# Part B of a gated two-branch kernel: projections over dense features, with copies between SBUF tiles for the heads

## The chip, the cores and the metric

The kernel runs on one core of one Trainium2 chip. The metric is the device time of one execution in microseconds. The engines are PE (TensorE, with its weight loads shown as PEld), DVE (VectorE), ACT (ScalarE), POOL (GpSimd) and SP (SyncE, which only issues DMAs and waits); ACT issues DMAs too. An engine runs its instructions in order, and so does the queue on which it issues DMAs: a command that waits holds everything behind it on that engine.

## The reference

Two branches over the same `x` (2048 tokens, 640 features) are mixed by a gate.

```python
g = sigmoid((x * gate_w).sum(-1, keepdims=True))
a = A_ref(x, mem0, Wq, Wk, Wv, Wo, seg_len)   # recurrent: 64 segments of 32 tokens, one after the other
b = B_ref(x, wqkv, wo)                        # local attention, dilated
return g * a + (1 - g) * b
```

Only B matters for the change. It has 32 heads of 20 features; each token attends to 8 tokens: itself and every second one before it.

```python
def B_ref(x, wqkv, wo):
    H, Dh, W, dil = 32, 20, 8, 2
    q, k, v = (x @ wqkv) split in three, then in H heads of Dh
    idx = pos[:, None] - (arange(W) * dil)[None, :]       # masked where negative
    logits = einsum('bhsd,bhswd->bhsw', q, k[idx]) * Dh ** -0.5
    attn = softmax(logits)
    o = einsum('bhsw,bhswd->bhsd', attn, v[idx])
    return o.reshape(B, S, 640) @ wo
```

## The kernel before

The program has three stages in this order: part B (`part_b`), a pre-pass for A (`prepass`), and the recurrent part A (`part_a`). Part B writes its result, already multiplied by `1 - g`, to DRAM; part A adds its own and stores the output.

**Part B.** The 2048 tokens are cut into five blocks `b`: four of 484 tokens (four chains `u` of 121 tokens of one parity, so that a dilated window is a band) and a last one of 112. Within a block the 32 heads are taken in eight groups `g` of four. Every array that a group needs has one head per 32 partitions, because PE addresses its tiles at multiples of 32: head `h` of a group lies in partitions 32h to 32h+19, and the other 12 are padding. To get there, the weights are padded: `wqk` holds each head's 20 columns in a slot of 32 (zeros behind them, built by POOL and DVE casts from a raw load), and `wop`, the output weight, has four heads' rows per slot (a POOL memset of the whole tile, then four DMAs of 20 rows).

One step of the loop at the end of `part_b` is one `(b, g)`:

- `proj` of the next group: five matmuls (the five chunks of 128 input features) give q of four padded heads, five more give k; DVE evicts q, ACT k, into `bqT` and `bkT` of three buffers each;
- `scores`: 16 small matmuls, an exp on ACT and a multiply by the band on DVE, in two halves;
- `values` of the group before: 16 matmuls for the sums and 16 for the weighted values; then Ln and Exp on ACT for the reciprocal, and a multiply on DVE that writes `OT`, the transposed output, in which each group again has its slot of 128 rows;
- from time to time `make_xT` (transposes x for the next 512 tokens, computes the gate, lets POOL copy two rearrangements `xh` and `zx` that SP stores to DRAM), `make_v` (v of the next block), and `out_tile`, the output projection of 128 tokens: eight matmuls, one per group, for each half of the columns, evicted by ACT and DVE and stored from ACT's queue.

**What sets the order.** Part B is ordered by a scheduler that places the program's instructions on each engine's list; within an engine and within a DMA queue that order is fixed. DMAs on SP and ACT share eight completion semaphores, taken in turn: a DMA waits until the one that last used its semaphore has landed. `load_early` puts eleven resident weights (`wres_q`, 384 KB each) and three DRAM-to-DRAM copies (`wscr`) on SP's queue after the first store of `xh`. Five streamed weights (`wst`) for the pre-pass follow at 58 us; once part B's buffers come free, `load_late` brings the rest (`wlate_*`). The pre-pass starts with `wres_q` and `wst` (L424).

The change touches L127 to L136 (weight loads and padding), `proj` (L213 to L224), one slice in `scores`, the end of `values` (L267 to L269), `out_tile` (L271 to L283) and the loop's order.

Of the kernel before, what the change touches and what calls it, by code (L numbers as in the profile page):

```python
# [10 lines left out]
BF = mybir.dt.bfloat16  # L11
# [4 lines left out]
N_LATE = 55  # L16
N_LATE2 = 22
WBUFS = 5

_DEV = {"mode": "full"}  # L20

# [3 lines left out]
class _K:  # L25
# [58 lines left out]
    def part_b(self):  # L84

        nc, tc, KC, S = self.nc, self.tc, self.KC, self.S
        NQ, HALO = 121, 14
        BQ = 4 * NQ
# [8 lines left out]
        with ExitStack() as ctx:  # L97
            wp = ctx.enter_context(tc.tile_pool(name="b_w", bufs=1))
            io = ctx.enter_context(tc.tile_pool(name="b_io", bufs=4))
            blkp = ctx.enter_context(tc.tile_pool(name="b_blk", bufs=1))  # L100
            wk = ctx.enter_context(tc.tile_pool(name="b_wk", bufs=2))
# [14 lines left out]
                load_x(i)  # L116
            wv = wp.tile([128, KC, 640], BF, name="wv_sb")
            gw = wp.tile([128, KC, 1], BF, name="gw_sb")
            wop = wp.tile([128, 8, 640], BF, name="wo_pad")
            wqk = [wp.tile([128, KC, 32, 32], BF, name=f"w{n}_pad") for n in "qk"]  # L120
            xT = wp.tile([128, KC, HALO + S], BF, name="xT")
            OT = wp.tile([128, 8, S], BF, name="OT")
            wsrc = self.wqkv.rearrange("(c p) f -> p c f", p=128)
            for n, w in enumerate(wqk):
                nc.gpsimd.memset(w[:, :, :, 20:32], 0.0)
                raw = OT[:].rearrange("p g t -> p (g t)")[:, 3200 * n:3200 * n + 3200]
                (nc.scalar, nc.sync)[n].dma_start(raw.rearrange("p (c f) -> p c f", c=KC), wsrc[:, :, 640 * n:640 * n + 640])  # L127
                for kc in range(KC):
                    eng = (nc.vector, nc.gpsimd)[(KC * n + kc) % 2]
                    eng.tensor_copy(w[:, kc, :, 0:20], raw[:, 640 * kc:640 * kc + 640].rearrange("p (h d) -> p h d", d=20))  # L130
            nc.sync.dma_start(gw[:], self.gate_w.rearrange("(c p o) -> p c o", p=128, o=1))
            nc.scalar.dma_start(wv[:], wsrc[:, :, 1280:1920])
            nc.gpsimd.memset(wop[:], 0.0)
            wosrc = self.wo.rearrange("(g h d) f -> h d g f", h=4, d=20)
            for hh in range(4):
                nc.sync.dma_start(wop[32 * hh:32 * hh + 20, :, :], wosrc[hh])  # L136
            ones = wp.tile([128, 32], BF, name="b_ones")
            nc.vector.memset(ones[:], 1.0)
            band = wp.tile([128, NQ], BF, name="band")
# [57 lines left out]
            def make_v(b):  # L197
                nq, nu, c0 = shape_of(b)
                nk = nq + 7
                for u in range(nu):  # L200
# [8 lines left out]
                        self.evac(V[0:nk, 320 * f:320 * f + 320], ps[0:nk, 0:320])  # L209
                    Vs[b, u] = V  # L210

            qk = {}

            def proj(b, g):
                nq, nu, c0 = shape_of(b)
                nt = nq * nu
                for n, (o0, nn) in enumerate(((c0 + HALO, nt), (c0, nt + HALO))):
                    ps = bank(F32, "ps_bqk")
                    for kc in range(KC):
                        nc.tensor.matmul(ps[:, 0:nn], lhsT=wqk[n][:, kc, 4 * g:4 * g + 4, :].rearrange("p h d -> p (h d)"),  # L220
                                         rhs=xT[:, kc, o0:o0 + nn], start=(kc == 0), stop=(kc == KC - 1))
                    t = wk.tile([128, BQ + HALO], BF, name="b" + "qk"[n] + "T", bufs=3)
                    self.evac(t[:, 0:nn], ps[:, 0:nn], "dve" if n == 0 else "act")
                    qk[b, g, n] = t  # L224

            Ps = {}

            def scores(b, g):
                nq, nu, c0 = shape_of(b)
                nk = nq + 7  # L230
                qT, kT = qk.pop((b, g, 0)), qk.pop((b, g, 1))
                for hp in range(2):
                    ps = psS.tile([128, 2, 512], F32, tag="S", name="ps_bS")
                    for u in range(nu):
                        a = 242 * (u // 2) + u % 2
                        for r in range(2):
                            rs = slice(64 * hp + 32 * r, 64 * hp + 32 * r + 32)
                            nc.tensor.matmul(ps[0:nk, r, nq * u:nq * u + nq], lhsT=kT[rs, a:a + 2 * nk - 1:2],
                                             rhs=qT[rs, a:a + 2 * nq - 1:2], start=(u == 0), stop=(u == nu - 1),
                                             tile_position=(64 * hp + 32 * r, 0), skip_group_check=True)  # L240
                    P = wk.tile([128, 2, BQ], BF, name="bP", bufs=4)
                    Pv = P[0:nk, :, 0:nq * nu]
                    nc.scalar.activation(Pv, ps[0:nk, :, 0:nq * nu], ACT.Exp, scale=scale_b)  # L243
                    P4 = Pv.rearrange("p r (u n) -> p r u n", n=nq)
                    m = band0[0:nk, 0:nu, 0:nq].unsqueeze(1) if b == 0 else \
                        band[0:nk, 0:nq].unsqueeze(1).unsqueeze(1)
                    nc.vector.tensor_tensor(out=P4, in0=P4, in1=m.to_broadcast([nk, 2, nu, nq]), op=ALU.mult)
                    Ps[b, g, hp] = P

            def values(b, g):  # L250
                nq, nu, c0 = shape_of(b)
                nk, nt = nq + 7, nq * nu
                po = psO.tile([128, 512], F32, tag="O", name="ps_bO")
                pz = psO.tile([128, 512], F32, tag="Z", name="ps_bZ")
                P = [Ps.pop((b, g, hp)) for hp in range(2)]
                for u in range(nu):
                    for out, z in ((pz, True), (po, False)):
                        for hh in range(4):
                            h = 4 * g + hh
                            nc.tensor.matmul(out[32 * hh:32 * hh + 32, nq * u:nq * u + nq],  # L260
                                             lhsT=ones[0:nk, :] if z else Vs[b, u][0:nk, 20 * h:20 * h + 32],
                                             rhs=P[hh // 2][0:nk, hh % 2, nq * u:nq * u + nq], start=(u == 0),
                                             stop=(u == nu - 1), tile_position=(0, 32 * hh), skip_group_check=True)
                rz = wk.tile([128, BQ], F32, name="b_rz")
                nc.scalar.activation(rz[:, 0:nt], pz[:, 0:nt], ACT.Ln)
                nc.scalar.activation(rz[:, 0:nt], rz[:, 0:nt], ACT.Exp, scale=-1.0)
                dst = OT[:, g, BQ * b:BQ * b + nt].rearrange("p (l n q) -> p l q n", l=nu // 2, q=2)  # L267
                nc.vector.tensor_tensor(out=dst, in0=po[:, 0:nt].rearrange("p (l q n) -> p l q n", q=2, n=nq),
                                        in1=rz[:, 0:nt].rearrange("p (l q n) -> p l q n", q=2, n=nq), op=ALU.mult)  # L269

            def out_tile(ti):  # L271
                bo = io.tile([128, 640], BF, name="bo", bufs=2)
                for f in range(2):
                    ps = bank(F32, "ps_bo")
                    for g in range(8):
                        nc.tensor.matmul(ps[:, 0:320], lhsT=OT[:, g, 128 * ti:128 * ti + 128],
                                         rhs=wop[:, g, 320 * f:320 * f + 320], start=(g == 0), stop=(g == 7))
                    if f == 0:
                        nc.scalar.activation(bo[:, 0:320], ps[:, 0:320], ACT.Copy, scale=self.omg_sb[:, ti:ti + 1])
                    else:  # L280
                        nc.vector.tensor_scalar(out=bo[:, 320:640], in0=ps[:, 0:320], scalar1=self.omg_sb[:, ti:ti + 1],
                                                scalar2=None, op0=ALU.mult)
                nc.scalar.dma_start(self.bsc_dram[ti * 128:(ti + 1) * 128, :], bo[:])  # L283

            nc.scalar.preload_act_table_set("natural_log_exp_and_others")
            steps = [(b, g) for b in range((S + BQ - 1) // BQ) for g in range(8)]
            self.first_store = None
            make_xT(0)
            with tc.issue_after(self.first_store):
                self.load_early()  # L290
            make_v(0)
            proj(*steps[0])
            ti = 0
            for i, (b, g) in enumerate(steps):
                if g == 2 and b + 1 < S // 512:
                    make_xT(b + 1)
                if (b, g) == (S // 512 - 1, 0):
# [4 lines left out]
                    for n in range(4):  # L302
                        for q in range(4):
                            nc.sync.dma_start(self.gZ[32 * q:32 * q + 32, n:n + 1],
                                                g_dram[:, 24:32, 4 * n + q:4 * n + q + 1])
                if g == 6 and i + 8 < len(steps):
                    make_v(b + 1)
                if i + 1 < len(steps):
                    proj(*steps[i + 1])
                scores(b, g)  # L310
                if i > 0:
                    values(*steps[i - 1])
                if g >= 1 and b > 0 and 128 * (ti + 1) <= BQ * b:
                    out_tile(ti)
                    ti += 1
            values(*steps[-1])
# [602 lines left out]
```

## Time and profile before

| | |
|---|---|
| median of 3 runs | 1776.31 us (1772.72 to 1780.4) |
| the profiled execution, span from first to last instruction | 1775.1 us; the page gives no other time for it |
| PE busy | 1674.0 us (94%) |
| ACT busy | 870.1 us (49%) |
| DVE busy | 651.2 us (37%) |
| POOL busy | 72.7 us (4%) |
| part B, to its last eviction | 0 to 225.6 us |
| pre-pass, then part A | from 225.6 us |

How to read it: the busy shares are means over the three stages, and only part B's are of use for the change, so the span is cut at part B's borders. A projection or a copy is priced by its own row there. SP is not in the list of busy engines, since all it does is issue and wait: its commands are found in the timeline of its queue (`SPq`), which gives the start and the duration of each group of commands. In lines of the trace, `out<-in` names the tiles.

### The profile page before, as it was taken

To read this page: it belongs to the slowest core of one execution; us is meant where nothing else is said; L and a number is where in the kernel's file an instruction comes from. 1 tells how busy PE (TensorE), PEld (TensorE's weight loads), DVE (VectorE), ACT (ScalarE), POOL (GpSimd) and SP (SyncE) were. 2 spreads that over 40 slices of the span, in tenths; PEclk is the share of its full clock that TensorE was granted. 3 is DMA by queue.
4 is the path that set the end of the run, shared out by engine and by line. 5 is a ranking of instruction groups with operands and counts; after the bars stand their busy time and mean duration, and the time that the engine had idled before them with its cause. 6 is when DMAs were issued, how large, how long until landed. Compare 5 with 4: busy or idle time off the path is not lost.

```text
span 1775.1 us, 82404 instructions
## 1 busy us (share of the span) xinstructions
PE 1674.0 (94%) x36512; PEld 997.3 (56%) x36527; DVE 651.2 (37%) x2047; ACT 870.1 (49%) x2377; POOL 72.7 (4%) x151
## 2 busy tenths in 40 slices
PE   6998999887999999999999999999999999999989
PEld 3554644334565655555556555555555556555557
DVE  4556533222333333333333333333333333333320
ACT  3766622223555555555555555555545555545550
POOL 4001000002000000000000000000000000000000
PEclk9999999998999999999999999999999999999999
DMA  6610195798899999999999999999999999989981
GB/s 164 203 32 29 46 315 171 207 283 233 293 301 307 305 300 301 300 299 304 300 294 304 308 293 308 298 297 297 305 292 299 301 297 304 303 289 300 299 282 30
DMA packets 280968, 461.12 MB, mean 260 GB/s; under 512 B 97188, under 2 KB 158116, under 8 KB 280612
## 3 DMA queue, kind: packets, MB, share of 16 engines
q1 hardware_dynamic: 173464, 395.75, 67.5%
q10 hardware_dynamic: 107148, 60.12, 11.9%
q8 instruction: 285, 4.67, 1.0%
q14 instruction: 71, 0.58, 0.1%
HBM read 421.44 MB, written 35.52 MB: 257 GB/s over the span
## 4 chain that ended last, share of the span: by engine, by line
PE 84%; ACT 6%; DMA 4%; issue 3%; DVE 2%; ACTq 1%; DVEq 0%
PE ps_qk L540 25%; PE ps_v L633 13%; PE ps_wo L697 11%; PE ps_qkT L557 6%; PE ps_pre L424 6%; PE ps_S L587 5%; PE ps_oT L656 3%; PE ps_z L851 3%; PE ps_bqk L220 3%; ACT bP L243 2%; DMA zpk_dram<-ZV 2%; ACT ZQ L778 2%; PE ps_mem L707 1%; PE ps_S L596 1%; PE ps_bv L207 1%
## 5 line engine op out<-in xcount | busy, mean ns | idle before, releaser
L549 ACT CAST KV<-ps_qk 128x384 bf16<-128x384 f32 x448 | 208.7, 480 | 340.2 <-PE ps_qk L540 196.5
L540 PEld LDWEIGHTS <-hT 128*32 128x32 bf16 x10240 | 247.7, 96 | 163.8 <-issue 21.0
L540 PE MATMUL ps_qk<-wlate_k,hT 128*32 128x384 bf16 x4352 | 270.0, 329 | 2.0 <-issue 2.0
L564 DVE COPY ZQ<-ps_qkT 128x384 bf16<-128x384 bf16 x256 | 91.6, 358 | 382.4 <-PE ps_qkT L557 216.8
L633 PE MATMUL ps_v<-wlate_v,hT 128*32 128x384 bf16 x4096 | 225.3, 330 | 0.0
L605 ACT ACTIVATE ZQ<-ps_S 32x224 bf16<-32x224 f32 x512 | 178.1, 348 | 43.7 <-PE ps_S L596 38.2
L697 PEld LDWEIGHTS <-KV 128*32 128x32 bf16 x6144 | 154.3, 96 | 67.0 <-issue 19.1
L540 PE MATMUL ps_qk<-wres_q,hT 128*32 128x384 bf16 x2816 | 164.2, 330 | 11.9 <-DMA hT<-in_A_mem_dram 10.7
L540 PE MATMUL ps_qk<-wst,hT 128*32 128x384 bf16 x1792 | 154.1, 328 | 0.6 <-DMA hT<-in_A_mem_dram 0.3
L633 PEld LDWEIGHTS <-hT 128*32 128x32 bf16 x5120 | 113.6, 96 | 66.8 <-issue 4.4
L697 PE MATMUL ps_wo<-wlate_oa,KV 128*32 128x384 bf16 x2560 | 140.4, 327 | 2.0 <-DVE ZQ L676 1.0
L587 PE MATMUL ps_S<-ZQ,KV 128*128 128x160 bf16 (+1 forms) x1024 | 136.9, 238 | 0.7 <-DMA ZQ<-zpk_dram 0.7
L697 PE MATMUL ps_wo<-wlate_ob,KV 128*32 128x256 bf16 x2688 | 124.2, 275 | 7.6 <-issue 7.5
L557 PE MATMUL ps_qkT<-ident,KV 128*128 128x128 bf16 x1536 | 130.0, 220 | 0.4 <-issue 0.4
L557 PEld LDWEIGHTS <-KV 128*128 128x128 bf16 x1536 | 89.0, 98 | 61.0 <-issue 40.8
L667 DVE CAST KV<-ps_oT 128x192 bf16<-128x192 f32 x256 | 79.2, 351 | 62.7 <-PE ps_oT L661 62.7
L587 PEld LDWEIGHTS <-KV 128*128 128x128 bf16 (+1 forms) x1024 | 58.8, 95 | 69.5 <-issue 42.2
L667 ACT CAST KV<-ps_oT 128x192 bf16<-128x192 f32 x256 | 69.6, 326 | 57.3 <-PE ps_oT L661 57.3
L710 DVE CAST hT<-ps_mem 128x24 bf16<-128x24 f32 x126 | 22.5, 179 | 199.1 <-PE ps_mem L707 199.1
L640 ACT CAST KV<-ps_v 128x384 bf16<-128x384 f32 x192 | 92.4, 481 | 3.3 <-PE ps_v L633 0.2
L633 PE MATMUL ps_v<-wst,hT 128*32 128x384 bf16 x1024 | 87.1, 330 | 2.4 <-DMA wst<-in_A_Wv_dram 2.4
L568 DVE COPY KV<-ps_qkT 128x384 bf16<-128x384 bf16 x256 | 89.0, 348 | 0.6 <-PE ps_qkT L557 0.4
(135 smaller groups left out, 2262.7 us busy)
## 6 DMA issues: line engine op xcount, KB each, us to landing
wst<-in_A_Wq_dram SPq DMA_DIRECT2D x260, 384.0 KB
wst<-in_A_Wv_dram SPq DMA_DIRECT2D x260, 384.0 KB
wst<-in_A_Wk_dram SPq DMA_DIRECT2D x195, 384.0 KB
wst<-wscr SPq DMA_DIRECT2D x192, 384.0 KB
zpk_dram<-ZS ACTq DMA_DIRECT2D x4, 3072.0 KB
ZQ<-zpk_dram ACTq DMA_DIRECT2D x64, 192.0 KB
wlate_k<-in_A_Wk_dram SPq DMA_DIRECT2D x17, 384.0 KB
wlate_v<-in_A_Wv_dram SPq DMA_DIRECT2D x16, 384.0 KB
```

The costliest lines, as they stand in the source:

```text
L424: nc.tensor.matmul(ps[:], lhsT=sls[kc][:, c0:c0 + 128], rhs=zT[:, kc, :], start=(kc == 0), stop=(kc == KC - 1))
L540: nc.tensor.matmul(pq[32 * j:32 * j + 32, 0:384], lhsT=hT[:, kc, :], rhs=sl[:, 384 * j:384 * j + 384], start=(kc == 0), stop=(kc == KC - 1 ...
L549: cp(sts[i], pqs[i][:, 0:384])
L557: nc.tensor.transpose(pT[:, t, :, :, :].rearrange("p j b i -> p (j b i)"), st[:, 128 * t:128 * t + 128], self.ident[:])
L564: nc.vector.tensor_copy(q_blocks(R)[:, 1:5, :, :].rearrange("p b c i -> p c b i"), pT.rearrange("p t j b i -> p (t j) b i"))
L568: nc.vector.tensor_copy(KV[:, 384 * (R % 2):384 * (R % 2) + 384], pT.rearrange("p t j b i -> p (t j b i)"))
L587: nc.tensor.matmul(grid(h, par)[:, :, 0:80].rearrange("p j (b r i) -> p j b r i", r=2, i=8)[:, :, :, r, :], lhsT=KT[k0:k1, 12 * r + c:12 * ...
L605: nc.scalar.activation(E[ps], pSs[h][ps, :, 112 * j:112 * j + 112], ACT.Exp, scale=scale_a)
L633: nc.tensor.matmul(pvs[R][32 * j:32 * j + 32, 0:384], lhsT=hT[:, kc, :], rhs=sl[:, 384 * j:384 * j + 384], start=(kc == 0), stop=(kc == KC ...
L640: cp(V[R], pvs[R][:, 0:384])
L667: cps[j % 2](oTxs[2 * h + j // 2][:, 6 * (j % 2):6 * (j % 2) + 6, :], pos[j][:, 0:240].rearrange("p (c q) -> p c q", q=40)[:, :, 8:40])
L697: nc.tensor.matmul(pso[part][32 * jj:32 * jj + 32, 0:n], lhsT=oTxs[2 * (R // 2) + j // 2][:, 6 * (j % 2) + 3 * (R % 2) + t, :], rhs=o_weig ...
```

## The change

`wqk` and `wo` are loaded as they are, dense: no padding, no casts, one DMA for the output weight. q and k are projected in five chunks `f` of 128 dense features instead of eight groups of padded heads. A chunk is evicted to a dense tile (`bqD`, `bkD`), and small DMAs on SP move each head's 20 rows to the partitions 32h of the group's tile (`bqT`, `bkT`, now four buffers). A head that lies across two chunks needs two DMAs. `values` writes a tile `boT` in the groups' layout, and DMAs on SP move its heads into the dense `OT`, over which the output projection runs five chunks. `scores` reads 20 rows of a slot, not 32.

The loop's order changes too: in a block's terms the chunks are projected at steps -2, -1, 1, 2 and 4, `make_v` moves from step 6 to step 5, and output tiles come from step 3 on.

```diff
+QKB = 4
...
-            wop = wp.tile([128, 8, 640], BF, name="wo_pad")
-            wqk = [wp.tile([128, KC, 32, 32], BF, name=f"w{n}_pad") for n in "qk"]
+            wo = wp.tile([128, KC, 640], BF, name="b_wo")
+            wqk = [wp.tile([128, KC, 640], BF, name=f"b_w{n}") for n in "qk"]
...
-            OT = wp.tile([128, 8, S], BF, name="OT")
+            OT = wp.tile([128, KC, S], BF, name="OT")
...
-            for n, w in enumerate(wqk):
-                nc.gpsimd.memset(w[:, :, :, 20:32], 0.0)
-                raw = OT[:].rearrange("p g t -> p (g t)")[:, 3200 * n:3200 * n + 3200]
-                (nc.scalar, nc.sync)[n].dma_start(raw.rearrange("p (c f) -> p c f", c=KC), wsrc[:, :, 640 * n:640 * n + 640])
-                for kc in range(KC):
-                    eng = (nc.vector, nc.gpsimd)[(KC * n + kc) % 2]
-                    eng.tensor_copy(w[:, kc, :, 0:20], raw[:, 640 * kc:640 * kc + 640].rearrange("p (h d) -> p h d", d=20))
+            nc.sync.dma_start(wqk[0][:], wsrc[:, :, 0:640])
+            nc.scalar.dma_start(wqk[1][:], wsrc[:, :, 640:1280])
...
-            nc.gpsimd.memset(wop[:], 0.0)
-            wosrc = self.wo.rearrange("(g h d) f -> h d g f", h=4, d=20)
-            for hh in range(4):
-                nc.sync.dma_start(wop[32 * hh:32 * hh + 20, :, :], wosrc[hh])
+            nc.sync.dma_start(wo[:], self.wo.rearrange("(c p) f -> p c f", p=128))
...
+            def pieces(g):
+
+                for hh in range(4):
+                    f = 80 * g + 20 * hh
+                    n = min(20, 128 - f % 128)
+                    yield 32 * hh, f // 128, f % 128, n
+                    if n < 20:
+                        yield 32 * hh + n, f // 128 + 1, 0, 20 - n
+
             qk = {}
 
-            def proj(b, g):
+            def proj(b, f):
...
-                        nc.tensor.matmul(ps[:, 0:nn], lhsT=wqk[n][:, kc, 4 * g:4 * g + 4, :].rearrange("p h d -> p (h d)"),
+                        nc.tensor.matmul(ps[:, 0:nn], lhsT=wqk[n][:, kc, 128 * f:128 * f + 128],
                                          rhs=xT[:, kc, o0:o0 + nn], start=(kc == 0), stop=(kc == KC - 1))
-                    t = wk.tile([128, BQ + HALO], BF, name="b" + "qk"[n] + "T", bufs=3)
+                    t = wk.tile([128, BQ + HALO], BF, name="b" + "qk"[n] + "D", bufs=2)
                     self.evac(t[:, 0:nn], ps[:, 0:nn], "dve" if n == 0 else "act")
-                    qk[b, g, n] = t
+                    for g in range(8):
+                        for p0, c, r0, nr in pieces(g):
+                            if c != f:
+                                continue
+                            if (b, g, n) not in qk:
+                                qk[b, g, n] = wk.tile([128, BQ + HALO], BF, name="b" + "qk"[n] + "T", bufs=QKB)
+                            nc.sync.dma_start(qk[b, g, n][p0:p0 + nr, 0:nn], t[r0:r0 + nr, 0:nn])
...
-                            rs = slice(64 * hp + 32 * r, 64 * hp + 32 * r + 32)
+                            rs = slice(64 * hp + 32 * r, 64 * hp + 32 * r + 20)
...
+                oT = wk.tile([128, BQ], BF, name="boT", bufs=3)
...
+                for p0, c, r0, nr in pieces(g):
+                    nc.sync.dma_start(OT[r0:r0 + nr, c, BQ * b:BQ * b + nt], oT[p0:p0 + nr, 0:nt])
...
-                    for g in range(8):
-                        nc.tensor.matmul(ps[:, 0:320], lhsT=OT[:, g, 128 * ti:128 * ti + 128],
-                                         rhs=wop[:, g, 320 * f:320 * f + 320], start=(g == 0), stop=(g == 7))
+                    for c in range(KC):
+                        nc.tensor.matmul(ps[:, 0:320], lhsT=OT[:, c, 128 * ti:128 * ti + 128],
+                                         rhs=wo[:, c, 320 * f:320 * f + 320], start=(c == 0), stop=(c == KC - 1))
...
+            projs = {8 * b + at: (b, f) for b in range((S + BQ - 1) // BQ)
+                     for f, at in enumerate((-2, -1, 1, 2, 4))}
...
+            proj(*projs[-2])
+            proj(*projs[-1])
             make_v(0)
-            proj(*steps[0])
...
-                if g == 6 and i + 8 < len(steps):
+                if g == 5 and i + 8 < len(steps):
                     make_v(b + 1)
-                if i + 1 < len(steps):
-                    proj(*steps[i + 1])
+                if i in projs:
+                    proj(*projs[i])
...
-                if g >= 1 and b > 0 and 128 * (ti + 1) <= BQ * b:
+                if g >= 3 and b > 0 and 128 * (ti + 1) <= BQ * b:
```

More of the change, by code (lines that the diff above doesn't have):

```diff
@@ L266, in values @@
                 nc.scalar.activation(rz[:, 0:nt], rz[:, 0:nt], ACT.Exp, scale=-1.0)
-                dst = OT[:, g, BQ * b:BQ * b + nt].rearrange("p (l n q) -> p l q n", l=nu // 2, q=2)
-                nc.vector.tensor_tensor(out=dst, in0=po[:, 0:nt].rearrange("p (l q n) -> p l q n", q=2, n=nq),
+                oT = wk.tile([128, BQ], BF, name="boT", bufs=3)
+                nc.vector.tensor_tensor(out=oT[:, 0:nt].rearrange("p (l n q) -> p l q n", l=nu // 2, q=2), in0=po[:, 0:nt].rearrange("p (l q n) -> p l q n", q=2, n=nq),
                                         in1=rz[:, 0:nt].rearrange("p (l q n) -> p l q n", q=2, n=nq), op=ALU.mult)
+                for p0, c, r0, nr in pieces(g):
+                    nc.sync.dma_start(OT[r0:r0 + nr, c, BQ * b:BQ * b + nt], oT[p0:p0 + nr, 0:nt])
             def out_tile(ti):
```

## The prediction

> **What bounds the kernel now.** First the page, for the share of each engine and whether the clock is throttled; then the busy time cut at part B's own borders (0 to 32 us: start; then one stretch for each of its five blocks; 225 us on: the pre-pass).
>
> ```profile
> span 1775.1 us, 82404 instructions
> ...
> PE   6998999887999999999999999999999999999989
> ```
>
> ```profile
> core 0: us, PE busy (x) PEld busy (x) DVE busy (x) ACT busy (x) POOL busy (x), PEclk, DMA share, GB/s
> ...
> 68.00:113.00 45.00, 41.24 (x595) 23.92 (x593) 25.99 (x45) 31.90 (x52) 3.54 (x7) 1.00 0.16 45
> 113.00:163.00 50.00, 44.07 (x614) 25.57 (x616) 31.27 (x48) 31.50 (x52) 8.88 (x8) 1.00 0.17 45
> 163.00:203.00 40.00, 35.38 (x553) 21.02 (x553) 22.17 (x37) 27.66 (x45) 0.21 (x2) 1.00 0.11 38
> 203.00:225.00 22.00, 21.70 (x364) 14.83 (x361) 11.66 (x39) 14.09 (x49) 0.00 (x0) 1.00 0.09 32
> ```
>
> Part B takes the first 225.6 us of 1775.1 and is bound by PE: 88 to 99% busy in its blocks, at the full clock. ACT has 30% to spare, and the transfers are nearly idle (0.09 to 0.17). So PE work removed here shortens the part, until the next limit. The chain of waits gives the price of that work, as pieces on the path:
>
> ```profile
> 59.56 2.09 PE ps_bqk L220 x10
> 66.49 2.19 PE ps_bqk L220 x10
> ...
> 82.61 2.17 PE ps_bo L276 x16
> ...
> 127.79 2.33 PE ps_bo L276 x16
> ```
>
> Ten projection matmuls (five for q, five for k) take 2.2 us; sixteen of the output 2.29 us. These chain pieces are the price; the mean durations by line are longer, because neighbours overlap.
>
> Then SyncE, which the change loads. The timeline of its queue (start, time taken by the commands, line, count):
>
> ```profile
> 20.77 1.52 SPq L136 DMA_DIRECT2D wo_pad<-in_B_wo_dram  x4
> 24.57 0.40 SPq L182 DMA_DIRECT2D xh_dram<-xh_blk  x1
> 28.54 0.64 SPq L187 DMA_DIRECT2D zT_dram<-zx_blk  x1
> 29.23 17.84 SPq L382 DMA_DIRECT2D wres_q<-in_A_Wq_dram  x11
> 47.12 4.27 SPq L370 DMA_DIRECT2D wscr<-in_A_Wo_dram  x3
> ...
> 129.02 1.13 SPq L298 DMA_DIRECT2D g_dram<-g_sb  x1
> 132.06 1.75 SPq L300 DMA_DIRECT2D gA<-g_dram  x4
> 133.86 12.44 SPq L304 DMA_DIRECT2D gZ<-g_dram  x16
> ```
>
> and single commands by their lines (ns: least, median, most):
>
> ```profile
> L136 SPq DMA_DIRECT2D wo_pad<-in_B_wo_dram x4: 301/354/358, 20.8 to 21.9; - x4
> L300 SPq DMA_DIRECT2D gA<-g_dram x4: 324/426/430, 132.1 to 133.4; - x4
> L304 SPq DMA_DIRECT2D gZ<-g_dram x16: 598/598/742, 133.9 to 145.7; - x16
> L283 ACTq DMA_DIRECT2D bsc_dram<-bo x16: 326/327/345, 76.7 to 225.6; - x16
> ```
>
> The reader is to see that one command occupies its queue for 0.30 to 0.60 us however little it moves (a gZ copy moves 128 bytes), and that in part B SyncE now issues about fifty commands, so this has cost nothing.
>
> **The change, part by part.**
>
> *Removed from PE.* Three of eight projection pairs a block: in four full blocks 12 x 2.2 = 26.4 us; in the short last block three pairs of about 0.7 us (its q and k chains last 0.4 us each, overlapping) = 2 us. Of the output, 6 of 16 matmuls for each of 16 tiles: 16 x 2.29 x 6/16 = 13.8 us. Together 42 us. ACT and DVE lose 15 of 40 evictions each (7.7 and 8.7 us), which lie under PE. At the start the ten weight casts on DVE and POOL and the 4.4 us memset of the padded weight go; SyncE's first 384 KB load, at 29.2 us, waits behind that POOL work, and I put it at about 18 us.
>
> *Added to SyncE.* Of 32 heads of 20 rows, four straddle a border of 128 features, so each tensor of a block needs 36 copies: 5 blocks x 3 tensors (q, k, output) x 36 = 540 commands (420 of 20 rows, 30 each of 4, 8, 12 and 16). The trace has no SBUF-to-SBUF copy, so their price is bounded by rows. Between two commands lie 0.05 us: sixteen gZ in 12.44 us, less one wait of 2.0 in the queue's waits, are 0.65 each, of which 0.60 is the command. Low: the shortest command, 0.30, plus 0.05: 0.35. High: gA's median, 0.43 + 0.05, so 0.47; beyond that gZ's 0.65. I take 0.40: the padded output weight, the only other copies of 20 rows, takes 1.52/4 = 0.38 each, and a little is added for the 4-row pieces, which might cost what gZ does. Data time is no limit: a copy moves under 20 KB, and the DMA share is 0.1.
>
> So 540 x 0.40 = 216 us of one in-order queue, 43 us a block. PE, with the change, needs 45 - 6.6 - 2.6 = 36 us in the second block, and some 17 us in the fifth, whose 108 copies are as many. The bound moves from PE to SyncE, and the 42 us are not collected.
>
> Here a rule of the Trainium skill can be weighed. The page "DMA: Bandwidth & Descriptors", section "Issuing engines are not separate DMA queues", says that the time a sequencer takes to initiate a DMA is usually small relative to the DMA itself. The wo_pad row does not bear that out for many small copies; by the rule the sum would be the first rival's.
>
> *Added waits.* Scores wait for copies, where they waited for an eviction: two hops more (an issue, a landing of about 2 us) for q and k and again for the output. Behind a waiting score stand, on PE, the values of the group before and the next output tile. The cover is the lead: q and k are projected two to four groups ahead, into four buffers where there were three, and a group's 13.5 copies take 5.4 us. The lead is worth nothing once SyncE itself is late, which is the forecast. That scores read 20 rows, not 32, changes no column count: nothing.
>
> *SyncE's own sum.* In the built program's order the first copy of q stands ahead of the eleven resident weight loads and three weight copies, all others behind them. Those fourteen took SyncE from 29.2 to 51.4 us, with a 10 us wait on input tiles that the new order does not have ahead of them; each command also waits for the one that used its semaphore eight places earlier. From 18 us, 14 transfers at 1.2 us plus a few us to land: the bulk of the copies begins at 37 us. Then:
> - 533 copies x 0.40 = 213 us;
> - the rest of the queue: three pairs of xh and zT stores (1.5 us each), g_dram with its landing (132.06 - 129.02 = 3.0), gA 1.9, gZ 10.3: 20 us;
> - waits at the head: the xh store of blocks 1 to 3 stands between copies and waits for make_xT and two POOL copies (1.8 + 0.8 us), 4 us each, or nothing where SyncE comes late: 12 us, with everything behind it held;
> - ACT's stores of output tiles wait on semaphores that SyncE's copies share, and hold exp and evictions behind them; between nothing and the 2.3 us of one output tile on PE for each of 16; nearer nothing, 0.5, because the stores are spread: 8 us;
> - at the end the last copy's landing (g_dram: 1.9 us) and one output tile (1.4 + 0.6): 4 us.
>
> 37 + 213 + 20 + 12 + 8 + 4 = 294 us where part B now ends at 225.6: 68 us later.
>
> *Moved.* Five streamed weight loads for the pre-pass, issued at 58 to 61 us now, stand behind all 586 earlier commands, in front of the resident late loads. They are issued while the last output tile runs; only the first is needed at once, and its landing (3 to 5 us after issue) is about the tail already counted. If that cover fails it costs 3 us. The late loads start today at 195.7 and mostly at 224.9 us, when part B's buffers come free; they keep their distance. The output tiles' later place (step 3 on) has PE slack above it. Pre-pass and part A are unchanged and move as a whole.
>
> Sum: 1775.1 + 68 = 1843 us. The page gives the span alone for its execution, 1.2 us under the median of the three runs (1776.31), so 1844 us.
>
> **The rivals.**
> 1. *Faster: the copies hide.* If a command between SBUF tiles costs much less than any row here, PE stays the bound and its 42 us count: 1776 - 42 = 1734 us. The turning point: 225.6 - 37 - 20 - 20 - 4 = 145 us for 533 copies, 0.27 us each; 0.19 for the whole gain. Against it: no row is under 0.30, on either queue, from 128 bytes to 384 KB. For it: no row is of this kind, and the page's rule above. 0.07.
> 2. *Dearer commands.* At the 0.47 us of gA, 533 x 0.07 = 37 us more: 1881 us; at gZ's 0.65 about 1975. For it: many rows are there. Against: the 20-row and the 128-row store rows (0.35, 0.33). 0.12.
> 3. *Landing, not issue.* Eight semaphores allow eight copies under way. Once a landing takes over 8 x 0.40 = 3.2 us, that sets the pace; at 4 us, 0.5 us a copy, 53 us more: 1897 us. g_dram landed 1.9 us after issue in the quiet stretch; only beside the bulk loads have I reason to expect more. Longer waits at the queue's head act the same way. 0.12.
> 4. *They cancel:* 0.3 us a copy and no waits at the head end within 9 us of before (a measurement of this kernel tells 0.5%, 9 us, from no change). 0.02.
>
> **How the numbers follow.** The forecast has what is left, 0.67. Its own range: at 0.375 without head waits and a start at 33 us the end is 257 us, 1808; with 0.43 and 15 us more of waits, 1875. The likeliest is 1844. The range for 8 in 10 goes down to 1800 (0.35 to 0.36 a copy) and up to 1895 (rivals 2 and 3 at their nearer ends), leaving out rival 1, no change, and the far ends. Faster by over 0.5%: 0.07; within: 0.02; slower: 0.91.
>
> **What would show it.** SyncE should be nearly always issuing between 37 and 290 us, 0.36 to 0.44 us from one copy to the next; PE's busy time should fall by some 40 us in part B while its idle time grows by 110; the first pre-pass matmul should start near 294 us, and from there to the end the length should stay 1549 us. Block 5 should last over 40 us, not 22. The prediction is wrong if copies follow each other in under 0.3 us, if SyncE idles while PE is full, or if the landing time, not the issue, spaces the copies.

## The result and the profile after

The changed kernel takes 2023.9 us (2021.69 to 2026.83, four runs) against 1776.81 us before: a ratio of 1.139, with an interval of 1.136 to 1.142. The forecast had the side and the mechanism, and far too small a size: 1844 us, at most 1895.

The page of the changed kernel, cut to the lines that answer to those of before, with the chain's shares added:

```profile
span 2021.0 us, 82814 instructions
...
PE   5765755347987999999999999999999999999999
...
PEclk8667666557999999999999999999999999999999
...
PE 71%; SPq 15%; DMA 6%; issue 3%; ACT 3%; ACTq 1%; DVE 1%; DVEq 0%
```

The same line of the kernel before:

```profile
PE 84%; ACT 6%; DMA 4%; issue 3%; DVE 2%; ACTq 1%; DVEq 0%
```

SyncE's queue (SPq), which was nowhere on the path, has 15% of it: some 300 us. Busy time in the five blocks of part B (cut where the scores of each block begin; the last stretch ends at the pre-pass):

```profile
core 0: us, PE busy (x) PEld busy (x) DVE busy (x) ACT busy (x) POOL busy (x), PEclk, DMA share, GB/s
...
32.00:115.00 83.00, 51.13 (x514) 24.61 (x514) 23.72 (x40) 29.38 (x44) 3.40 (x7) 0.62 0.22 62
115.00:200.00 85.00, 55.16 (x545) 27.40 (x545) 24.05 (x41) 31.46 (x48) 3.39 (x7) 0.66 0.18 46
200.00:286.00 86.00, 58.57 (x554) 28.34 (x554) 28.15 (x43) 31.65 (x48) 8.03 (x6) 0.68 0.18 48
286.00:381.00 95.00, 48.61 (x494) 24.19 (x495) 21.24 (x36) 29.22 (x43) 0.00 (x0) 0.61 0.11 27
381.00:470.00 89.00, 32.69 (x262) 15.98 (x261) 9.45 (x32) 12.64 (x40) 0.00 (x0) 0.52 0.07 17
```

No engine of the list is full, the blocks have become about equally long, 83 to 95 us, whatever work is in them (the last has 112 tokens and took 22 us before), and the granted clock (PEclk), 1.00 before, is 0.52 to 0.68. What is full is the queue that the list does not have. Its timeline, at the start and at the end of the copies:

```profile
27.51 4.13 SPq L383 DMA_DIRECT2D wscr<-in_A_Wo_dram  x3
31.69 6.26 SPq L232 DMA_DIRECT2D bqT<-bqD  x6
38.06 5.18 SPq L232 DMA_DIRECT2D bkT<-bkD  x7
43.34 5.09 SPq L232 DMA_DIRECT2D bqT<-bqD  x7
...
450.65 17.14 SPq L279 DMA_DIRECT2D OT<-boT  x23
467.83 2.15 SPq L395 DMA_DIRECT2D wst<-in_A_Wq_dram  x4
```

Seven copies in 5.18 us, 23 in 17.14: 0.74 us each, and the next group starts 0.1 us after. Single commands by their lines (ns):

```profile
L232 SPq DMA_DIRECT2D bqT<-bqD x180: 554/708/2368, 16.9 to 444.6; - x180
L232 SPq DMA_DIRECT2D bkT<-bkD x180: 554/707/1026, 38.1 to 449.8; - x180
L279 SPq DMA_DIRECT2D OT<-boT x180: 554/708/1622, 66.1 to 467.1; - x180
```

The command itself occupies SyncE for 0.71 us, twice the padded weight's 0.35. The chain of waits in the last block, by line, leaves little else than these two lines:

```profile
by line: SPq L232 46.4%; SPq L279 38.6%; issue 7.0%; DMA bkT<-bkD 4.0%; DMA wst<-in_A_Wq_dram 3.9%; ACT bP L251 0.8%; PE ps_bS L246 0.7%; DVE bP L255 0.6%
```

The first matmuls of the pre-pass, before and after:

```profile
L424 PE MATMUL ps_pre<-zT,wres_q x128: 379/379/389, 225.6 to 263.8; 128*128 128x512 bf16 x128
...
L437 PE MATMUL ps_pre<-zT,wres_q x128: 379/379/634, 470.5 to 511.1; 128*128 128x512 bf16 x128
```

The pre-pass begins at 470.5 us for 225.6, 244.9 later; from there to the end it is 1550.4 us for 1549.6. All of the loss lies in part B.

### The profile page after: what moved, and what is told of

It reads as the page before. It is cut to its first block, busy times and chain, and to the rows that moved or that the text cites. A ratio compares the mean times of both kernels' runs of the same rounds, so it can differ in the third digit from the quotient of the medians.

```text
span 2021.0 us, 82814 instructions
## 1 busy us (share of the span) xinstructions
PE 1744.4 (86%) x36266; PEld 1012.8 (50%) x36281; DVE 638.2 (32%) x2027; ACT 871.8 (43%) x2362; POOL 60.5 (3%) x143
## 4 chain that ended last, share of the span: by engine, by line
PE 71%; SPq 15%; DMA 6%; issue 3%; ACT 3%; ACTq 1%; DVE 1%; DVEq 0%
PE ps_qk L553 22%; PE ps_v L646 11%; PE ps_wo L710 10%; SPq L232 10%; PE ps_pre L437 5%; PE ps_qkT L570 5%; PE ps_S L600 4%; SPq L279 4%; PE ps_oT L669 3%; PE ps_z L864 2%; DMA bkT<-bkD 2%; ACT ZQ L791 1%; PE ps_pre L451 1%; DMA zpk_dram<-ZV 1%; PE ps_mem L720 1%
## 5 line engine op out<-in xcount | busy, mean ns | idle before, releaser
L246 PE MATMUL ps_bS<-bqT,bkT 20*128 20x121 bf16 (+1 forms) x576 | 58.6, 271 | 119.7 <-DMA bkT<-bkD 118.3
L251 ACT ACTIVATE bP<-ps_bS 128x968 bf16<-128x968 f32 (+1 forms) x80 | 67.9, 853 | 210.0 <-PE ps_bS L246 208.5
L246 PEld LDWEIGHTS <-bkT 20*128 20x128 bf16 (+1 forms) x576 | 30.2, 114 | 178.1 <-DMA bkT<-bkD 136.1
```

## The experiments

Each run is told against the kernel before in the same set of runs (medians 1774 to 1778 us).

**A price list of commands.** The kernel before, with copies that nobody reads, in stretches where SyncE is idle; sixteen forms, four of each (two shown).

```diff
+            def prices1(q):
+                nc.vector.tensor_copy(pS[0:20, 0:484], q)
...
+                for i in range(4):
+                    nc.sync.dma_start(pD[0][0:20, i, 0:484], pS[0:20, 0:484])
...
+            def prices2(q):
+                nc.vector.tensor_copy(pS[0:20, 0:484], q)
...
+                for i in range(4):
+                    nc.sync.dma_start(pD[0][0:20, i, 0:484], pX[i, 0:20, 0:484])
...
+                if (b, g) == (1, 3):
+                    prices1(qk[b, g, 0][0:20, 0:484])
+                if (b, g) == (3, 1):
+                    prices2(qk[b, g, 0][0:20, 0:484])
```

> The kernel before, plus 64 extra copies that nobody reads, put on SyncE's queue where it is idle (blocks 1 and 3): four each of sixteen forms, so that the price of one command can be read by its form. The output is the reference's. Theory A (the command itself is dear): 20 rows of 968 bytes between SBUF tiles occupy SyncE for about 0.71 us, 16 rows for 0.55, 12 for 0.72, 8 for 0.65, 4 for 0.62, as in the changed kernel; 32, 64 and 128 rows cost about as little as 16, because their count divides by 16; and 20 rows from DRAM cost 0.35 as the padded output weight did. Rival B (the commands were slow because so many were under way and the semaphores were short): the same 20-row copy, in a queue that is otherwise empty, costs 0.35 to 0.40. Both: the time stays within 0.5% of before, since PE does not wait for any of them.

Measured: 1767.97 us in its one run, 0.4% under before. `prS` and `prD` are SBUF tiles, `prX` lies in DRAM; ns, least, median, most. In order: between SBUF tiles 4, 8, 12, 16, 20, 32 and 128 rows of 968 bytes; 20 and 16 rows to DRAM; 20 and 16 rows from DRAM; between SBUF tiles 20 rows of 1024 and of 320 bytes.

```profile
L159 SPq DMA_DIRECT2D prD<-prS x4: 577/597/939, 84.3 to 86.6; - x4
L161 SPq DMA_DIRECT2D prD<-prS x4: 624/624/638, 87.2 to 89.3; - x4
L163 SPq DMA_DIRECT2D prD<-prS x4: 714/721/759, 90.0 to 92.4; - x4
L165 SPq DMA_DIRECT2D prD<-prS x4: 566/592/1147, 93.2 to 95.6; - x4
L167 SPq DMA_DIRECT2D prD<-prS x4: 706/724/768, 96.2 to 98.6; - x4
L169 SPq DMA_DIRECT2D prD<-prS x4: 554/586/589, 99.3 to 101.2; - x4
...
L173 SPq DMA_DIRECT2D prD<-prS x4: 595/599/600, 104.4 to 106.3; - x4
L178 SPq DMA_DIRECT2D prX<-prS x4: 303/322/690, 164.2 to 165.6; - x4
L180 SPq DMA_DIRECT2D prX<-prS x4: 312/419/1425, 166.0 to 168.3; - x4
L182 SPq DMA_DIRECT2D prD<-prX x4: 323/328/355, 168.7 to 169.9; - x4
L184 SPq DMA_DIRECT2D prD<-prX x4: 314/418/418, 170.3 to 171.5; - x4
L186 SPq DMA_DIRECT2D prD<-prS x4: 710/726/791, 172.0 to 174.4; - x4
L188 SPq DMA_DIRECT2D prD<-prS x4: 706/707/1298, 175.2 to 178.0; - x4
```

Theory A holds and rival B falls: in a queue that is otherwise empty the 20-row copy costs 0.72 us. What sets the price is neither bytes (320 or 1024 a row: 0.71, 0.73) nor rows (128 rows: 0.60), but above all where the ends lie: both in SBUF 0.59 to 0.73 here, one in DRAM 0.32 to 0.33 for 20 rows and 0.42 for 16. That holds for copies of this form, a row for each partition. The gZ commands (32 rows of 4 bytes, out of DRAM) cost 0.60 all the same, so the pattern of a copy counts as well as its ends. A second, smaller part between SBUF tiles depends on the row count: 4, 8, 16, 32 and 128 rows cost 0.59 to 0.62, 12 and 20 rows 0.72.

**q and k alone** (the output as before: padded, eight chains).

```diff
+                dst = OT[:, g, BQ * b:BQ * b + nt].rearrange("p (l n q) -> p l q n", l=nu // 2, q=2)
...
-                for p0, c, r0, nr in pieces(g):
-                    nc.sync.dma_start(OT[r0:r0 + nr, c, BQ * b:BQ * b + nt], oT[p0:p0 + nr, 0:nt])
...
-                    for c in range(KC):
+                    for g in range(8):
```

> The change for q and k alone: the output keeps its padded layout and eight chains, so 360 of the 540 copies are left. Theory A (SyncE's commands set part B, 0.755 us from one copy to the next): part B ends near 32 + 360 x 0.755 + 22 = 326 us, the time is about 1876 us. Rival C (PE's lower granted clock, 0.53 to 0.82, is what makes part B long): PE has 14 us more work than in the changed kernel, so the time does not fall in proportion to the copies and stays above 1980 us.

Measured: 1894.43 us, ratio 1.068 (1.066 to 1.070); pre-pass from 338.4 us. 180 copies fewer are worth 470.5 - 338.4 = 132 us, 0.73 a copy, although PE has more to do. This is theory A's outcome, 18 us over its number; rival C's bound of 1980 us is missed by far.

**The output alone** (q and k as before; output tiles from step 3 on, as in the change).

```diff
-                dst = OT[:, g, BQ * b:BQ * b + nt].rearrange("p (l n q) -> p l q n", l=nu // 2, q=2)
...
+                oT = wk.tile([128, BQ], BF, name="boT", bufs=3)
...
+                for p0, c, r0, nr in pieces(g):
+                    nc.sync.dma_start(OT[r0:r0 + nr, c, BQ * b:BQ * b + nt], oT[p0:p0 + nr, 0:nt])
```

> The change for the output alone: q and k keep their padded weights and eight chains, 180 copies are left, 36 a block. Theory A: 36 x 0.755 = 27 us a block fit under PE's 37 to 50 us in the four full blocks, so SyncE is not the limit there and the 14 us of output matmuls are saved; in the short last block SyncE needs 27 us where PE needs about 17, which gives back some 5 to 8 us. Time 1766 to 1772 us. Rival D (each hop through a copy costs its latency on the path, whatever the queue's load): 40 hops of about 2 us, the time rises to 1800 us or more.

Measured: 1789.78 us, ratio 1.010 (1.008 to 1.012): between the two expectations. Its third and its last block, and the end of its chain of waits (from 219.4 us on, the pieces that it lists before these lines are copies on SyncE):

```profile
112.00:163.00 51.00, 43.69 (x581) 23.83 (x584) 31.68 (x46) 30.80 (x51) 9.21 (x8) 0.93 0.22 57
...
199.00:238.00 39.00, 22.50 (x344) 13.62 (x340) 12.07 (x40) 15.05 (x50) 0.00 (x0) 0.77 0.12 31
```

```profile
233.74 0.71 SPq L277
234.49 0.71 SPq L277
235.24 1.76 DMA OT<-boT
237.05 0.73 PE ps_bo L284 x2
```

The last block lasts 39 us for 22.6, twice the loss that was allowed for. And the four full blocks, where SyncE has room, take 169.9 us (from their first scores at 29.5 to the last block's at 199.4) for 171.1 before: of 11 output tiles' 0.86 us each, 9.5 us, one arrives. The fourth block has all of its share (36.6 us for 40.0); the second and third lose it (45.3 for 44.7, 51.2 for 49.6). Of the 8 us lost, some 5 are longer busy time of PE (149.8 us in the four blocks for 154.0, where 9.5 less were due) and 3 are waits. The lower clock has part of it: in the third block PE waits 3.4 us for an eviction behind a DVE multiply of 4.9 us, and its granted clock is 0.50 from 138.1 to 144.9 us. Before, the same wait was 2.6 us and the clock stayed at 1.00. Whether the copies or the output tiles' later steps bring these waits about, this run can't tell apart.

**k's copies on ACT's queue.**

```diff
-                            nc.sync.dma_start(qk[b, g, n][p0:p0 + nr, 0:nn], t[r0:r0 + nr, 0:nn])
+                            (nc.sync, nc.scalar)[n].dma_start(qk[b, g, n][p0:p0 + nr, 0:nn], t[r0:r0 + nr, 0:nn])
```

> The changed kernel with the 180 copies of k issued from ACT's queue, the other 360 from SyncE's. Theory A: a queue pays for its own commands only, so SyncE's part falls to 32 + 360 x 0.755 + 22 = 326 us; ACT has 168 us of work in part B and takes 180 x 0.755 = 136 us more, 304 in all, still less. Time 1876 to 1910 us. Rival B (landings and the eight semaphores that both queues share set the pace): the copies are as many, so the time stays near 2020 us.

Measured: 1921.95 us, ratio 1.084 (1.081 to 1.086), 12 us above theory A's band and 100 below rival B. The lines of the copies, and what waited on them:

```profile
L232 SPq DMA_DIRECT2D bqT<-bqD x180: 554/710/1514, 17.6 to 348.9; - x180
L232 ACTq DMA_DIRECT2D bkT<-bkD x180: 561/722/1399, 19.6 to 343.0; - x180
...
  ACT bP L251: 114.0, 17
```

A queue pays for its own commands, and the price on ACT is the same. There they hold up the exp of the scores (`bP`): 17 times, 114 us of ACT standing idle in all.

**Rows in multiples of 16.** Padding rows take further rows of the chunk.

```diff
-                            nc.sync.dma_start(qk[b, g, n][p0:p0 + nr, 0:nn], t[r0:r0 + nr, 0:nn])
+                            fit = min(32 - p0 % 32, 128 - r0) // 16 * 16
+                            m = fit if fit >= nr else nr
+                            nc.sync.dma_start(qk[b, g, n][p0:p0 + m, 0:nn], t[r0:r0 + m, 0:nn])
```

> The changed kernel, in which copies of q and k move 32 or 16 rows instead of 20, 12, 8 or 4 wherever rows of the dense chunk and of the head's slot allow it (300 of 360; the further rows land in the slot's padding, which nobody reads). As many commands, more bytes. Theory A (the command's own price, which the price list puts at 0.55 to 0.59 us where the row count divides by 16 and at 0.71 for 20 rows): 300 x 0.12 to 0.15 = 36 to 45 us less, about 1980 to 1988 us. Rival B (landings set the pace): more bytes per copy, so no gain, 2020 us or more.

Measured: 1990.96 us in its one run, 33 us under the changed kernel; pre-pass from 441.4. More bytes in as many commands are faster, as theory A says, 3 us outside its band.

**Every copy through DRAM.**

```diff
+                    d = self.dram.tile([128, BQ + HALO], BF, name=f"qk_dram{n}_{b}_{f}")
+                    nc.sync.dma_start(d[:, 0:nn], t[:, 0:nn])
...
-                            nc.sync.dma_start(qk[b, g, n][p0:p0 + nr, 0:nn], t[r0:r0 + nr, 0:nn])
+                            nc.sync.dma_start(qk[b, g, n][p0:p0 + nr, 0:nn], d[r0:r0 + nr, 0:nn])
...
-                    nc.sync.dma_start(OT[r0:r0 + nr, c, BQ * b:BQ * b + nt], oT[p0:p0 + nr, 0:nt])
...
+                    nc.sync.dma_start(od[b, c][r0:r0 + nr, 0:nt], oT[p0:p0 + nr, 0:nt])
+                    if r0 + nr == 128:
+                        nc.sync.dma_start(OT[:, c, BQ * b:BQ * b + nt], od[b, c][:, 0:nt])
```

> The changed kernel with every copy having one end in DRAM: an evicted chunk is stored to DRAM by one copy and its heads are read from there, 20 rows at a time; the output's heads are stored to DRAM and each chunk is read back by one copy. 540 small copies as before, and 75 large ones more. Theory A' (a command is dear because both ends lie in SBUF; the price list has 0.32 us for 20 rows with an end in DRAM): 615 x 0.37 = 228 us, part B ends near 32 + 228 + 22 = 282 us, or up to 50 us later if SyncE stands at the head of its queue for each store that is read back at once. Time 1832 to 1882 us: that is where the prediction's sum, made with 0.40 us a copy, lay. Rival (the number of commands or hops sets the time, whatever their ends): 2024 us or more.

Measured: 1898.26 us, ratio 1.069 (1.065 to 1.073). More commands, and 126 us faster than the changed kernel: the number of commands or hops alone does not set the time.

```profile
L234 SPq DMA_DIRECT2D bqT<-qk_dram x180: 240/328/1509, 37.9 to 327.8; - x180
```

At 0.33 us, 0.37 from one to the next, the price is near the 0.40 that I had assumed in the prediction, and the end (pre-pass from 345.5) is still 14 us past the top of the expectation. Part of that is the start, with the first scores at 50.8 us for 40.0 in the changed kernel. After it SyncE is no longer full, and the chain of waits passes through the projections (22.5% of 103 to 226 us), at a PE clock of 0.56 to 0.75.

**Few commands through DRAM.** Nine loads for a tensor and block, each with a group's four heads; output padded (first run), or through DRAM too (second run).

```diff
+                    nc.sync.dma_start(d[128 * f:128 * f + 128, 0:nn], t[:, 0:nn])
...
+                        src = d[80 * g:80 * g + 32, 0:nn]
+                        nc.sync.dma_start(w[0:32 * nh, 0:nn], bass.AP(
+                            tensor=src.tensor, offset=src.offset,
+                            ap=[[20 * src.ap[0][0], nh], list(src.ap[0]), list(src.ap[1])]))
```

> q and k dense as in the change, moved through DRAM with few commands: five stores of 128 rows and nine loads per tensor and block (one load brings a group's four heads, 32 overlapping rows each), 140 commands in all of part B for 360; the output keeps its padded layout. Theory A': 140 x 0.5 = 70 us of commands and some 50 us of waits for stores fit under PE, which keeps its 28 us of removed projections less about 8 us at the start, where the first chunks stand behind the bulk loads: 1752 to 1766 us, faster than both kernels. Rival D (the hops' latency, about 5 us a chunk, lies on the path): 1776 us or more.

> As the run before, and the output dense too, through DRAM: eight stores of a group and thirteen loads a block, 245 commands in all. Theory A': SyncE has 245 x 0.5 = 122 us of commands, 25 us of them in the short last block where PE needs 17; PE saves 42 us in all. 1742 to 1768 us. Rival D: 1776 us or more.

Measured: 1816.95 us, ratio 1.024 (1.020 to 1.027), and 1849.62 us, ratio 1.041 (1.037 to 1.044). Theory A' fails in both, and the times are rival D's. Two blocks of the first, which took 44 and 50 us before, and a wait of the scores in 88 to 240 us:

```profile
89.00:141.00 52.00, 43.46 (x562) 22.92 (x552) 23.65 (x41) 29.97 (x48) 3.52 (x7) 0.81 0.34 101
141.00:199.00 58.00, 44.51 (x578) 25.06 (x578) 26.14 (x43) 30.01 (x48) 9.17 (x8) 0.84 0.33 95
```

```profile
PEld L259 <- DMA bkT<-qk_dram: 27.6, 11, 5.1
```

Nothing is full here. PE waits in pieces of up to 5.1 us for keys, and the granted clock is 0.81 to 0.84 on average, so that PE is busy as long as before with less to do. But waits in the blocks are not all: of the first run's 39 us in part B, 15 are lost ahead of the first scores (47.0 us for 31.8), where the first stores to DRAM stand behind the bulk loads on SyncE, 23 in the full blocks and 1 in the last. An order that lets these stores go first was not tried.

**More matmuls, to keep PE's clock up.** Twelve a step in the changed kernel, five in the first DRAM kernel; nobody reads them.

```diff
+                fill = bank(F32, "ps_fill")
+                for _ in range(12):
+                    nc.tensor.matmul(fill[:, 0:484], lhsT=wqk[0][:, 0, 0:128], rhs=xT[:, 0, HALO:HALO + 484],
+                                     start=True, stop=True, skip_group_check=True)
                 scores(b, g)
```

> The changed kernel with 12 more matmuls in each of the 40 steps, whose result nobody reads, so that PE idles less and its granted clock in part B (0.53 to 0.82) comes nearer to 1. Theory A (SyncE's commands set part B): the clock rises, and the time stays at 2024 us within 15 us. Rival C (the lower clock is part of the loss): with the clock back the time falls by more than 20 us, although PE has some 100 us more work.

> The run with q and k through DRAM (1817 us), with 5 more idle matmuls in each step. There SyncE is not full and PE waits in short pieces, at a clock of 0.77 to 0.86. Theory E (the hops' waits cost twice, once as waits and again as a slower PE): with the clock nearer 1 the time falls to 1795 to 1812 us, although 40 us of matmuls are added. Rival D (the waits alone): the added work does not fit into the waits, 1817 us or more.

Measured: 2027.36 and 1839.97 us. The first and the last block of the changed kernel with them:

```profile
32.00:115.00 83.00, 57.63 (x571) 28.13 (x573) 21.46 (x38) 28.30 (x42) 3.12 (x3) 0.83 0.22 60
...
381.00:470.00 89.00, 50.57 (x351) 20.64 (x351) 10.51 (x33) 12.82 (x40) 0.00 (x0) 0.67 0.09 26
```

The clock rises from 0.62 to 0.83 and from 0.52 to 0.67, PE is busy 62 us longer, and the pre-pass starts at 468.6 us for 470.5. In the changed kernel the lower clock costs no time; rival C is out. In the DRAM kernel the clock rises too (0.88 to 1.00 from the second block on), but the time rises as well, by 23 us. Theory E falls; of the 40 us of matmuls that the expectation counts as added, only a part fits into the waits.

**The output alone, last block padded** (output tiles from step 2 on).

```diff
+                last = BQ * b + nt == S
+                oT = OTp[:, g, 16:128] if last else wk.tile([128, BQ], BF, name="boT", bufs=3)
...
+                if last:
+                    return
+                if BQ * b + nt == S - 112:
+                    nc.gpsimd.tensor_copy(OTp[:, g, 0:16], oT[:, nt - 16:nt])
```

> The change for the output alone, without the short last block: blocks 1 to 4 go through the 144 copies into a dense output and five chains; the last 112 tokens, and 16 before them, keep the padded layout and eight chains, so that no copy stands at the end. Theory A: the copies lie under PE in the full blocks, as in the run with the output alone, and the 16 us that its last block lost are not lost: 1765 to 1772 us, faster than both kernels by a little. Rival D (latency or the queue's head still cost in the full blocks): 1776 us or more.

Measured: 1792.91 us, ratio 1.010 (1.008 to 1.013). Theory A fails again: without copies at the end, the first four blocks take 180.6 us (33.9 to 214.5) for 171.1. PE is busy in them for 159.3 us, for 154.0 before, with 66 matmuls of the output fewer, and the granted clock is below 1.00 in three of the four. One of them:

```profile
113.00:163.00 50.00, 41.92 (x561) 21.81 (x560) 31.12 (x43) 30.21 (x49) 9.42 (x8) 0.90 0.25 63
```

So the lower clock takes part in this loss; what brings it on is open here too. No kernel with copies for the heads beats the one before.

## Why the prediction was right or wrong

**Right: the bound.** It moves from PE to SyncE's issue. The queue is full from 31.7 us on (all but 3 of 436 us are commands and the gaps of some 0.05 us between them), the blocks are about equally long, the pre-pass shifts as a whole, and its length stays (1550.4 us for 1549.6). Taking copies away (132 us for 180) and making them cheaper (33 us by row counts) moved the time; 62 us more of PE's busy time did not.

**Wrong: "I take 0.40".** That term of the sum is the failing step. The sum beside what the trace has:

| term | predicted, us | measured, us | difference |
|---|---|---|---|
| bulk of the copies begins | 37 | 31.7 | -5 |
| the copies after that | 533 x 0.40 = 213 | 539 x 0.766 = 413 | +200 |
| rest of the queue | 20 | 21 | +1 |
| waits at the queue's head | 12 + 8 | 3 | -17 |
| the tail | 4 | 2.7 | -1 |
| part B's end | 294 | 470.5 | +177 |

(0.766 is the commands' 381.9 us with their share of the 32 us between commands, by 539. The prediction's 533 is a slip of 2 us: one copy stands ahead of the bulk loads, not seven.) The row was chosen by its row count, 20, as though that were what the copies had in common with it; a command of the padded weight moves eight rows for each of 20 partitions. The price list shows that the ends matter: the padded weight comes from DRAM, and 20 rows from DRAM still cost 0.33, between SBUF tiles 0.72. I had written that the trace holds no such copy, and yet let the range end at 0.47; the gZ row, 0.65 with its gap, was named and left out, and even that would have been too low.

**Rival 2 (dearer commands)** is what happened, beyond its far end of 0.65 and 1975 us, and it had a chance of 0.12 in all. **Rival 3 (landing)** did not set the pace: a command is 0.71 us long without any wait, and the same in an empty queue. **Rival 1** stood on the turning point of 0.27 us a copy. The copies that came nearest, 0.37 through DRAM, did not turn it, and the run with 28 commands a block, far under that load, was slower than before as well. So the rival's premise, that PE's 42 us count as soon as SyncE has room, is not borne out either: with q and k through DRAM PE waits for keys, and with the output alone 1.2 of 9.5 us arrive. There the prediction's cover, a lead of two to four groups, was too thin for hops through DRAM; a longer lead was not tried. How the output alone loses its 8 us is settled in part: some 5 us are PE's longer busy time, with a lower clock in one block, and 3 are waits. What starts them is not shown.

**The rule weighed there.** The page "DMA: Bandwidth & Descriptors" of the Trainium skill ("Issuing engines are not separate DMA queues") has the initiation of a DMA as usually small relative to the DMA. Here a copy of 19 KB takes 0.71 us to initiate and lands some 1.9 us after that (copies of k in the changed kernel's chain of waits): that is not small, and 540 such commands set the time. What that section says of several issuing engines, that they save the sequencer's time, is what the run with k on ACT shows (1922 us for 2024).

**Head waits (-17)** were overrated because SyncE comes late everywhere, which the prediction had given as the case in which they cost nothing. The weights queued behind 586 commands were hidden by the tail, as forecast: the first pre-pass matmul starts 2.7 us after the first of them is issued.

**PE's busy time** was to fall by 40 us in part B; it rose by 70 (1744.4 us for 1674.0), though 246 matmuls went. A weighted value's matmul (`ps_bO`) takes 275 ns for 217 and an output matmul 410 for 300, at the lower clock. The forecast had no term for the clock, and for the changed kernel's time it did not need one.

## What to carry to other kernels

Before moving data in small pieces, price one command on its queue and multiply: an issuing engine is an engine, even if the list of busy times leaves it out, and here 36 commands of 0.75 us filled 27 us, though each moved under 20 KB. A price is taken from a row whose two ends lie in the same memories and whose pattern is the same; where the trace has none, the range goes to the dearest row and beyond, since one small run with a price list would decide it. And room in the queue is not enough: with q and k through DRAM SyncE had room, and PE's saved time still went into waits for hops that ended after the step that reads them was due.

## What the runs showed of the hardware

- One command between SBUF tiles took 0.55 to 0.75 us of its queue, with one end in DRAM 0.32 to 0.33 for the same 20 rows; 128 rows cost less (0.60) than 12 (0.72). An end in DRAM did not make every form cheap: a gZ command took 0.60, a load of four heads at once 0.53, one of 100 or 120 rows of the output 0.77. The page "DMA: Bandwidth & Descriptors" of the Trainium skill ("Why a DMA increments its semaphore by 16 and not by 1") says that the largest number up to 16 that divides the rows gives the engines used, and that the sequencer itself writes the missing increments when they are fewer. The step from 0.59 at 16, 32 and 128 rows to 0.72 at 12 and 20 agrees with such an extra write. The 0.60 and 0.62 for 4 and 8 rows, which would need it too, hardly do, and the 0.33 for 20 rows from DRAM, cheaper than 16 rows (0.42), does not. Why two ends in SBUF are dearer stays open.
- PE's granted clock followed its waits: 1.00 at 88 to 99% busy, 0.81 to 0.84 with waits of up to 5 us, 0.52 to 0.68 when it waited for SyncE, and up again with idle matmuls. The page "TensorE: Matmul & The Clock Gate" of the Trainium skill ("Part 1") describes such a gate, driven by how busy PE has been. On the busy line such a PE looks fuller than its work is: in part B it was busy for 263.9 us, where 193.7 us did for more matmuls before.
- The kernel with the price list ran 1767.97 us once, with a part A 9 us shorter than before (1540.2 us for 1549.6 from the pre-pass on), which nothing in its edit touches and which stays unexplained. So differences of 0.5% between builds are not read here.
